# Attention and two expert layers on one core: outer products on other PSUM partitions, wider products for the rest of q, fewer identity products, a new list

## The chip, the cores and the metric

The kernel runs on one core of a Trainium2 chip, in one launch. The metric is the device time of the launch in microseconds (us), lower is better. TensorE (PE in the profile) multiplies, VectorE (DVE), ScalarE (ACT) and GpSimd (POOL) work on elements, and SyncE (SP) issues nearly all transfers from and to HBM, in one queue, in order. Each engine works through its own list of instructions in order and waits for the others by semaphores.

## The reference

```python
# q, k, v: (4, 8, 576, 64); moe_w1, moe_w2: (512, 1024); moe_w3: (1024, 1024); moe_w_out: (1024, 512)
# experts: e_w1 (4, 512, 1024), e_w2 (4, 1024, 512); probs (2304, 4)
kv  = einsum('bhsd,bhse->bhde', k, v)
out = einsum('bhsd,bhde->bhse', q, kv)
out = out / sqrt(mean(out * out, axis=-1) + 1e-6) * g_norm
x = out.transpose(0, 2, 1, 3).reshape(2304, 512)
x = ((x @ w1) * (x @ w2) @ w3) @ w_out
p = probs / (probs.sum(-1, keepdims=True) + 1e-9)
y = sum over e of p[:, e] * (maximum(x @ e_w1[e], 0) @ e_w2[e])
```

The weights of the middle layer arrive as 64-bit floats, as pairs of 32-bit words, and are decoded on ScalarE and VectorE.

## The kernel before

**Attention.** There are 16 *units*, `unit b p`: two heads of one batch. A unit loads q (256 KB) and k and v (288 KB each for batches 0 and 1, which are listed in `NINE`; 256 KB each for batches 2 and 3, and small loads `kvr` of the last 64 tokens). Its steps on TensorE are: outer products k by v (L756 for batches 0 and 1, 18 products; L769 for batches 2 and 3, 12 products), four transposes of q (L724), an inner product of four matmuls of q with the outer product (L804), and, after a normalization, four transposes of the result (L724 again, `ident,x`). Between them ScalarE or VectorE copies the outer products to a tile `kvb` with one block for each head on its diagonal (L788), copies the turned q (L712, L713), squares and sums (L622 or L626, L632); GpSimd takes the root (L639); VectorE scales (L643). In L756 head h uses rows and output partitions 64h to 64h+63. In L769 all 128 rows are tokens, and both heads write partitions 0 to 63, at different columns of the bank:

```python
nc.tensor.matmul(
    ps[0:D, h * D:(h + 1) * D], a, b_, start=r == 0 and h == 0, stop=r == R + 1,
    skip_group_check=True,
)
```

`EARLY` lists the results (in the order of the list) whose squares ScalarE makes in one instruction, with the sum on VectorE; all others are squared and summed on ScalarE in eight pieces of 64 columns.

**Rest of q.** `rest_unit g` does the last 64 tokens of two batches: for each of eight heads and two batches one product of 64 columns with weights of 128 columns (L840), 16 in all.

**Later stages.** The middle layer uses block products of fewer multiplications (`bilinear_plain`, `bilinear_pair`, `mixed_product`, `mixed`); the expert layers follow (L1763 and the three passes of L341 to L343, which multiply float32 numbers split in a high and a low part).

**What sets the order.** `FRONT` is a list of items, written out; each gives operations with an engine and a cost. A planner (`Plan.order`) runs these against modelled engines: the item's place in the list is its priority, an operation is taken when its inputs are ready by the model and a tile is free, and where ScalarE or VectorE could do it, the one that would finish first gets it. So the list and the costs (`cost=` of a load, `{"pe": 1.4}` of the outer products) together fix each engine's order. `FILL` puts products of the identity with itself (L2027) into a fresh PSUM bank, ahead of TensorE's next operation of the stages 1 to 3; `WARM` is the number of such products ahead of everything (L438).

Of the kernel before, what the change touches and what calls it, by code (L numbers as in the profile page):

```python
# [18 lines left out]
P = 128  # L19
# [12 lines left out]
NINE = (0, 1)  # L32
TRAFFIC = 1.02
MARGIN = {"act": 0.1, "dve": 0.1, "sp": 0.2}
EARLY = (2, 3, 4, 5, 8, 15, 16)
WARM = 10
FILL = {1: 3, 2: 3, 3: 2}
START = 0.7
RESERVE = {"h": (5, 2), "b": (1, 1)}
BIAS = {"dve": 1.0, "act": 0.0, "pool": 1.0, "pe": 0.0, "sp": 0.0}  # L40

FRONT = (
# [12 lines left out]
)  # L55

class Buf:
# [210 lines left out]
def attention_moe_kernel(  # L268
# [26 lines left out]
    nc = tc.nc  # L295
# [166 lines left out]
    def decode(name, src, shape=None):  # L462

        raw = Buf("r", name + "raw", [P, 512], I64)
        load(raw, ((lambda t: t.rearrange("p (k f) -> p k f", k=shape)) if shape else whole, src))
        val, add_ = half("val", ring="decoded"), half("add", I32, "decoded")  # L470

        def word(i):
            return raw.tile.bitcast(I32).rearrange("p (n t) -> p n t", t=2)[:, :, i]

        def magnitude(e):
            if e == "act":
                nc.scalar.activation(out=val.tile, in_=word(1).bitcast(F32), func=ACTF.Abs)
            else:
                nc.vector.tensor_scalar(
                    out=val.tile.bitcast(I32), in0=word(1), scalar1=0x7FFFFFFF, scalar2=None, op0=ALU.bitwise_and  # L480
                )

        def rounded(e):
            low = word(0).bitcast(U32)
            if e == "act":
                nc.scalar.activation(out=add_.tile, in_=low, func=ACTF.Copy, scale=2.0 ** -29)
            else:
                nc.vector.tensor_scalar(out=add_.tile, in0=low, scalar1=2.0 ** -29, scalar2=None, op0=ALU.mult)

        def bounded(e):  # L490
            nc.vector.tensor_scalar(
                out=val.tile, in0=val.tile, scalar1=as_float(0x38000000), scalar2=as_float(0x47EFFFFF),
                op0=ALU.max, op1=ALU.min,
            )

        def shifted(e):
            bits = val.tile.bitcast(I32)
            nc.vector.tensor_scalar(
                out=bits, in0=bits, scalar1=3, scalar2=0x3FFFFFFF,
                op0=ALU.logical_shift_left, op1=ALU.bitwise_and,  # L500
            )

        def signed(e):
            bits = val.tile.bitcast(I32)
            nc.vector.scalar_tensor_tensor(
                out=bits, in0=word(1), scalar=-0x40000000, in1=bits, op0=ALU.bitwise_and, op1=ALU.bitwise_or
            )

        def finish(e):
            bits = val.tile.bitcast(I32)  # L510
            nc.vector.tensor_tensor(out=bits, in0=bits, in1=add_.tile, op=ALU.add)

        either = {"act": t_act(512), "dve": t_fast(512)}
        add(either, magnitude, reads=[raw], writes=[val])
        add(either, rounded, reads=[raw], writes=[add_])
        add({"dve": t_fast(512)}, bounded, writes=[val])
        add({"dve": t_fast(512)}, shifted, writes=[val])
        add({"dve": t_dve(512)}, signed, reads=[raw], writes=[val])
        add({"dve": t_dve(512)}, finish, reads=[add_], writes=[val])
        return val  # L520
# [67 lines left out]
    def rest_kv(b, j):  # L588

        turn = sum(at[1] == j for at in kvr) % 2  # L590
        if (turn, j) not in kvr_slots:
            kvr_slots[turn, j] = [half("kvr") for _ in (k, v)]
            for raw in kvr_slots[turn, j]:
                for at in ((REM // 2, REM), (REM, P)):
                    cleared(raw, at)
        kvr[b, j] = kvr_slots[turn, j]
        for raw, src in zip(kvr[b, j], (k, v)):
            load(
                raw,
                (  # L600
                    lambda t: t[0:REM // 2].rearrange("p (h r d) -> p h r d", h=HP, r=2),
                    src[b, j * HP:(j + 1) * HP, M:S, :].rearrange("h (p r) d -> p h r d", r=2),
                ),
                key=0, cost=0.33,
            )

    summed = []
# [121 lines left out]
    def unit(b, p):  # L729
# [3 lines left out]
        loaded = []  # L733
        for name, src in (("q", q), ("kv", k), ("kv", v))[:1 if b in NINE else 3]:
            raw = half(name, ring="attention")
            load(raw, (heads, head_pair(src, b, p)), cost=0.8)
            loaded.append(raw)
        qraw = loaded[0]
        if b in NINE:
            kv = Buf("r", "kv", [P, 2, S], F32)  # L740
            load(kv, *(
                (lambda t, n=n: t[:, n], src[b, 2 * p:2 * p + 2].rearrange("h (g r) d -> (h g) (r d)", g=D))
                for n, src in enumerate((k, v))
            ), cost=1.72)
        else:
            ks, vs = loaded[1:]
            if (b, p // 2) not in kvr:
                rest_kv(b, p // 2)
            kr, vr = kvr[b, p // 2]
# [11 lines left out]
        def outer(e):  # L761
            for r in range(R + 2):
                for h in range(2):
                    if r < R:
                        a, b_ = heads(ks.tile)[:, h, r, :], heads(vs.tile)[:, h, r, :]
                    else:
                        at = (p % 2 * 2 + h) * 2 * D + (r - R) * D
                        a, b_ = kr[:, at:at + D], vr[:, at:at + D]
                    nc.tensor.matmul(  # L769
                        ps[0:D, h * D:(h + 1) * D], a, b_, start=r == 0 and h == 0, stop=r == R + 1,  # L770
                        skip_group_check=True,
                    )

        if b in NINE:
            add({"pe": 1.4}, outer_by_head, reads=[kv], writes=[ps])
        else:
            add({"pe": 0.9}, outer, reads=[ks, vs, kr, vr], writes=[ps])
        own, at = kvb[b][p // 2], p % 2 * 2 * P
        parts = []
        for i in range(2):  # L780
            for h in range(2) if b in NINE else (None,):
                d = slice(i * D, (i + 1) * D)
                n, heads_of = (P, slice(0, 2)) if h is None else (D, slice(h, h + 1))
                rows = slice(0, D) if h is None else slice(h * D, (h + 1) * D)
                parts.append((own, (p, i, h)))
                add(
                    {"act": t_act(n, True), "dve": t_dve(n)},
                    lambda e, d=d, heads_of=heads_of, rows=rows: (  # L788
                        nc.scalar.copy if e == "act" else nc.vector.tensor_copy
                    )(  # L790
                        own[d, at:at + 2 * P].rearrange("p (h c) -> p h c", h=2)[:, heads_of, d],
                        ps[rows, 0:P].rearrange("p (h c) -> p h c", h=2)[:, heads_of],
                    ),
                    reads=[ps], writes=parts[-1:], free=True,
                )
# [18 lines left out]
    def rest_unit(g):  # L814
# [18 lines left out]
        po = bank()  # L833

        def inner(e):
            for h in range(H):
                c = slice(h // 2 * P, (h // 2 + 1) * P)
                for i in range(2):
                    own, at = kvb[2 * g + i][h // 4], h % 4 * P + h % 2 * D
                    nc.tensor.matmul(  # L840
                        po[:, h * D:(h + 1) * D], qs[i][:, c], own[:, at:at + D], start=i == 0, stop=i == 1
                    )

        add({"pe": 1.72}, inner, reads=qs + kvb[2 * g] + kvb[2 * g + 1], writes=[po])
# [1215 lines left out]
```

## Time and profile before

| what | us |
|---|---|
| median of three runs (1115.97 to 1116.68) | 1116.59 |
| profiled execution | 1114.81 |
| its span in the trace | 1113.0 |
| TensorE busy | 1106.1 |
| VectorE busy | 864.4 |
| ScalarE busy | 607.3 |

The span runs from the first to the last instruction of the profiled execution; some 1.8 us lie around it. Records of TensorE overlap (each contains the time in which a product runs through the array), so its busy time tells little, and starts tell when it really issued. A float32 product shows as two records, a transpose as one. A number in brackets behind a row of the list in time is idle time ahead of it and what ended it.

### The profile page before, as it was taken

The page shows a single profiled execution, that of the slowest core. Times are in us where ns is not written, and L with a number is a line of the kernel's source. Part 1 is how long each engine was busy: PE and PEld are TensorE (multiplying, and loading weights), DVE is VectorE, ACT ScalarE, POOL GpSimd, SP SyncE. Part 2 cuts the span into 40 slices and gives each one's busy share as a digit, 9 for nine tenths or more (in the row PEclk, how much of TensorE's full clock was granted, in tenths as well). Part 3 has the DMA queues.
Part 4 walks back from the last instruction along what each step waited for, and adds up shares of the span by engine and source line. Part 5 has one row for each costly group of instructions (what it writes and reads, how often), then busy time and mean ns, then how long its engine had stood idle before and what let it go on. Part 6 is the DMA issues. An engine that isn't in the chain of part 4 may idle for free.

```text
span 1113.0 us, 18828 instructions
## 1 busy us (share of the span) xinstructions
PE 1106.1 (99%) x6577; PEld 1008.8 (91%) x6577; DVE 864.4 (78%) x1692; ACT 607.3 (55%) x1401; POOL 50.9 (5%) x69
## 2 busy tenths in 40 slices
PE   9999999999999999999999999999999999999998
PEld 8888888888888898999989999999999999999998
DVE  4778888988898888888888884567788876485896
ACT  6887636645655665763555465444455555444431
POOL 5521100000000000000000000000000000000000
PEclk9999999999999999999999999999999999999999
DMA  9888979542340399997999997878779967686756
GB/s 316 275 263 266 325 253 331 169 130 79 90 138 1 140 302 339 359 323 256 360 347 350 354 326 268 296 233 295 223 240 338 320 225 249 235 288 221 263 166 196
DMA packets 158723, 282.32 MB, mean 254 GB/s; under 512 B 17316, under 2 KB 65444, under 8 KB 158628
## 3 DMA queue, kind: packets, MB, share of 16 engines
q1 hardware_dynamic: 158464, 280.85, 75.3%
q8 instruction: 52, 0.85, 0.3%
q10 hardware_dynamic: 164, 0.26, 0.1%
q14 instruction: 43, 0.35, 0.1%
HBM read 198.22 MB, written 82.84 MB: 253 GB/s over the span
## 4 chain that ended last, share of the span: by engine, by line
PE 99%; DVE 0%; ACT 0%; issue 0%; POOL 0%; POOLq 0%
PE b L343 25%; PE b L341 25%; PE b L342 25%; PE b L1763 18%; PE b L724 2%; PE b L804 1%; PE b L769 1%; PE b L756 1%; PE b L840 1%; PE b L2027 1%; PE warm L438 0%; ACT x L626 0%; DVE acc L1881 0%; DVE htl L391 0%; DVE acc L1791 0%
## 5 line engine op out<-in xcount | busy, mean ns | idle before, releaser
L712 ACT COPY u<-b 128x384 f32<-128x384 f32 (+1 forms) x193 | 97.9, 507 | 212.6 <-PE b L343 207.1
L1763 PE MATMUL b<-w,hth 128*128 128x512 f32 x588 | 208.4, 394 | 0.1
L1599 DVE TENSOR_TENSOR u<-u,b 128x384 f32<-128x384 f32 x144 | 79.4, 552 | 110.9 <-PE b L343 53.2
L1763 PE MATMUL b<-w,htl 128*128 128x256 f32 x588 | 156.0, 279 | 0.0
L1763 PEld LDWEIGHTS b<-w,hth 128*128 128x128 f32 x588 | 108.9, 188 | 19.7 <-DVE acc L1791 0.5
L1763 PEld LDWEIGHTS b<-w,htl 128*128 128x128 f32 x588 | 110.6, 188 | 3.0
L1791 DVE SCALAR_TENSOR_TENSOR acc<-b,pn,acc 128x512 f32<-128x512 f32 x123 | 85.5, 746 | 29.7 <-PE b L1763 29.5
L386 ACT CAST hth<-s 128x384 fp32r<-128x384 f32 x144 | 69.7, 512 | 44.0 <-DVE s L1699 42.7
L1610 ACT ACTIVATE u<-u 128x384 f32<-128x384 f32 x108 | 56.9, 527 | 45.7 <-DVE u L1599 45.6
L391 DVE TENSOR_TENSOR htl<-s,hth 128x384 fp32r<-128x384 f32 x144 | 75.6, 552 | 5.3 <-ACT hth L386 5.2
L391 DVE TENSOR_TENSOR htl<-u,hth 128x384 fp32r<-128x384 f32 x108 | 56.0, 552 | 3.2 <-ACT hth L386 3.2
L343 PE MATMUL b<-wdh,htl 128*128 128x512 f32 x144 | 56.7, 394 | 0.0
L342 PE MATMUL b<-wdl,hth 128*128 128x512 f32 x144 | 56.6, 393 | 0.0
L341 PE MATMUL b<-wdh,hth 128*128 128x512 f32 x144 | 56.0, 389 | 0.0
L386 ACT CAST hth<-u 128x384 fp32r<-128x384 f32 x107 | 51.2, 509 | 0.4
L341 PE MATMUL b<-w,hth 128*128 128x256 f32 x168 | 47.8, 285 | 0.5 <-DMA w<-w2kept 0.4
L342 PE MATMUL b<-w,hth 128*128 128x256 f32 x168 | 47.5, 283 | 0.0
L343 PE MATMUL b<-w,htl 128*128 128x256 f32 x168 | 47.5, 283 | 0.0
L341 PE MATMUL b<-th,weh 128*128 128x512 f32 x112 | 43.8, 391 | 0.0
L342 PE MATMUL b<-tl,weh 128*128 128x512 f32 x112 | 43.7, 390 | 0.0
L343 PE MATMUL b<-th,wel 128*128 128x512 f32 x112 | 43.6, 389 | 0.0
L1053 DVE TENSOR_TENSOR u<-u,b 128x512 f32<-128x512 f32 x42 | 28.7, 686 | 17.9 <-PE b L343 10.3
(304 smaller groups left out, 3176.4 us busy)
## 6 DMA issues: line engine op xcount, KB each, us to landing
w<-w2kept SPq DMA_DIRECT2D x126, 512.0 KB, 4.9
we<-we SPq DMA_DIRECT2D x240, 256.0 KB, 5.1
we<-weh SPq DMA_DIRECT2D x48, 256.0 KB, 3.8
we<-wel SPq DMA_DIRECT2D x48, 256.0 KB, 3.5
e2raw<-in_moe_w_dram SPq DMA_DIRECT2D x20, 512.0 KB, 5.7
w3raw<-in_moe_w_dram SPq DMA_DIRECT2D x16, 512.0 KB, 3.7
e1raw<-in_moe_w_dram SPq DMA_DIRECT2D x16, 512.0 KB, 5.6
w2kept<-wth SPq DMA_DIRECT2D x32, 256.0 KB, 3.9
```

The lines of the kernel that those rows point to most:

```text
L341: nc.tensor.matmul(ps, w[0], x[0], start=first, stop=False, skip_group_check=more)
L342: nc.tensor.matmul(ps, w[0], x[1], start=False, stop=False, skip_group_check=more)
L343: nc.tensor.matmul(ps, w[1], x[0], start=False, stop=last, skip_group_check=more)
L386: nc.scalar.copy(to(dst.high.tile), value(src.tile))
L391: nc.vector.tensor_tensor(out=to(dst.low.tile), in0=value(src.tile), in1=to(dst.high.tile), op=ALU.subtract)
L712: lambda e: nc.scalar.copy(to(dst.tile), value(src.tile)) if e == "act"
L724: nc.tensor.transpose(ps[:, c], raw[:, c], ident)
L1053: lambda _: nc.vector.tensor_tensor(out=t.tile, in0=t.tile, in1=ps.tile, op=ALU.add),
L1599: lambda _: nc.vector.tensor_tensor(out=t[:, :W], in0=base[:, :W], in1=ps[:, :W], op=ALU.add),
L1610: lambda eng: nc.scalar.activation(out=t[:, :W], in_=src[:, :W], func=ACTF.Relu)
L1763: nc.tensor.matmul(ps.tile if whole_width else ps[:, 0:256], (h.high if whole_width else h.low)[:, c], both if whole_width else raw[:, r, ...
L1791: nc.vector.scalar_tensor_tensor(out=a.tile, in0=ps.tile, scalar=sc, in1=a.tile, op0=ALU.mult, op1=ALU.add)
```

## The change

Five things are edited. The outer products of batches 2 and 3 write head h to output partitions 64h to 64h+63 (`ps[c, c]`), as those of batches 0 and 1 did; all units now share one form of the copies to `kvb`, four of 64x64. `rest_unit` takes two heads at once: 8 products of 128 columns, whose right operand is two blocks of `kvb` at a distance. `FILL` is empty and `WARM` is 7. `EARLY` has ten entries. `FRONT` is a new list, and four planner costs are other numbers (a load of a 64-bit weight 1.4 instead of 1.5, of k and v of a unit of batches 0 and 1 1.53 instead of 1.72, and so on).

```diff
-EARLY = (2, 3, 4, 5, 8, 15, 16)
-WARM = 10
-FILL = {1: 3, 2: 3, 3: 2}
+EARLY = (1, 2, 3, 4, 5, 6, 7, 8, 9, 15)
+WARM = 7
+FILL = {}
 FRONT = (
-    "norm_scale, unit 1 2, unit 1 3, weight 1 4, unit 1 1, weight 1 0, unit 1 0, unit 0 1, unit 0 2, unit "
+    "norm_scale, unit 1 2, weight 1 4, unit 1 0, unit 1 1, weight 1 0, unit 1 3, unit 0 0, unit 0 1, unit "
...
-                    nc.tensor.matmul(
-                        ps[0:D, h * D:(h + 1) * D], a, b_, start=r == 0 and h == 0, stop=r == R + 1,
-                        skip_group_check=True,
-                    )
+                    c = slice(h * D, (h + 1) * D)
+                    nc.tensor.matmul(ps[c, c], a, b_, start=r == 0, stop=r == R + 1)
 
         if b in NINE:
-            add({"pe": 1.4}, outer_by_head, reads=[kv], writes=[ps])
+            add({"pe": 1.27}, outer_by_head, reads=[kv], writes=[ps])
...
-        for i in range(2):
-            for h in range(2) if b in NINE else (None,):
-                d = slice(i * D, (i + 1) * D)
-                n, heads_of = (P, slice(0, 2)) if h is None else (D, slice(h, h + 1))
-                rows = slice(0, D) if h is None else slice(h * D, (h + 1) * D)
-                parts.append((own, (p, i, h)))
+        for h in range(2):
+            for i in range(2):
+                rows, src = slice(i * D, (i + 1) * D), slice(h * D, (h + 1) * D)
+                dst = slice(at + h * P + i * D, at + h * P + (i + 1) * D)
+                parts.append((own, (p, h, i)))
...
-            for h in range(H):
-                c = slice(h // 2 * P, (h // 2 + 1) * P)
+            for h in range(HP):
+                c = slice(h * P, (h + 1) * P)
                 for i in range(2):
-                    own, at = kvb[2 * g + i][h // 4], h % 4 * P + h % 2 * D
+                    own, at = kvb[2 * g + i][h // 2], h % 2 * 2 * P
                     nc.tensor.matmul(
-                        po[:, h * D:(h + 1) * D], qs[i][:, c], own[:, at:at + D], start=i == 0, stop=i == 1
+                        po[:, c], qs[i][:, c],
+                        own[:, at:at + 2 * P].rearrange("p (b c) -> p b c", c=D)[:, 0:4:3], start=i == 0, stop=i == 1,
                     )
```

Lines behind the edits move: L769 is L770 in the changed kernel, L788 is L785, L804 is L798, L840 is L834.

TensorE at the start of the program, before (the names are output<-operands; `q_103` and `kv_107` belong to unit 1 2, `q_116` and `kv_121` to unit 1 3, `q_170` to unit 1 1):

```order
L438 MATMUL warm_86<-ident_72 128x128 x10
L2027 MATMUL b_124<-ident_72 128x128 x3
L724 MATMUL b_124<-ident_72,q_103 128x128 x4
L1950 MATMUL b_137<-ident_72,graw_76 128x1
L2027 MATMUL b_144<-ident_72 128x128 x3
L756 MATMUL b_144<-kv_107 64x64 x18
L2027 MATMUL b_172<-ident_72 128x128 x3
L724 MATMUL b_172<-ident_72,q_116 128x128 x4
L2027 MATMUL b_192<-ident_72 128x128 x3
L756 MATMUL b_192<-kv_121 64x64 x18
L2027 MATMUL b_217<-ident_72 128x128 x3
L804 MATMUL b_217<-kvb_99,qt_135 128x128 x4
```

and with the change (`q_100`, `kv_104`: unit 1 2; `q_125`, `kv_130`: unit 1 0; `q_161`, `kv_166`: unit 1 1; `q_227`: unit 1 3):

```order
L438 MATMUL warm_86<-ident_72 128x128 x7
L724 MATMUL b_118<-ident_72,q_100 128x128 x4
L1945 MATMUL b_135<-ident_72,graw_76 128x1
L756 MATMUL b_137<-kv_104 64x64 x18
L724 MATMUL b_173<-ident_72,q_125 128x128 x4
L798 MATMUL b_185<-kvb_96,qt_127 128x128 x4
L756 MATMUL b_196<-kv_130 64x64 x18
L724 MATMUL b_229<-ident_72,q_161 128x128 x4
L756 MATMUL b_242<-kv_166 64x64 x18
L798 MATMUL b_271<-kvb_94,qt_194 128x128 x4
L724 MATMUL b_283<-ident_72,q_227 128x128 x4
```

The identity groups between the units' groups are gone, and unit 1 0 stands second instead of unit 1 3.

SyncE's queue of loads at the start, before (`q_103`, `q_116`, `q_170`: as above; `w2raw_139` is `weight 1 4`):

```order
L363 DMA q_103<-in_q_dram 128x2x256
L363 DMA kv_107<-in_k_dram 128x576
L363 DMA kv_107<-in_v_dram 128x576
L363 DMA q_116<-in_q_dram 128x2x256
L363 DMA kv_121<-in_k_dram 128x576
L363 DMA kv_121<-in_v_dram 128x576
L363 DMA w2raw_139<-in_moe_w2_dram 128x2x256
L363 DMA q_170<-in_q_dram 128x2x256
```

and with the change (`w2raw_113`: `weight 1 4`; `q_125`: unit 1 0; `q_161`: unit 1 1):

```order
L363 DMA q_100<-in_q_dram 128x2x256
L363 DMA kv_104<-in_k_dram 128x576
L363 DMA kv_104<-in_v_dram 128x576
L363 DMA w2raw_113<-in_moe_w2_dram 128x2x256
L363 DMA q_125<-in_q_dram 128x2x256
L363 DMA kv_130<-in_k_dram 128x576
L363 DMA kv_130<-in_v_dram 128x576
L363 DMA q_161<-in_q_dram 128x2x256
```

The first weight moves from behind the second unit's loads to ahead of them.

## Rows read from the trace of the kernel before

**Rows 1.** The page's busy times: us (share of the span) and instructions.

```profile
PE 1106.1 (99%) x6577; PEld 1008.8 (91%) x6577; DVE 864.4 (78%) x1692; ACT 607.3 (55%) x1401; POOL 50.9 (5%) x69
```

**Rows 2.** TensorE's waits, whole span: for whom, total us, times, longest us.

```profile
PE warm L438 <- POOL ident masks.py:199: 1.3, 1, 1.3
PE b L804 <- ACT kvb L788: 0.6, 1, 0.6
PE b L341 <- DMA w<-w2kept: 0.4, 1, 0.4
```

**Rows 3.** TensorE in order of time, 0 to 45 us: start, us, what, records.

```profile
1.34 4.51 PE L438 MATMUL warm<-ident 128*128 128x128 f32 x20 [1.34 <-POOL ident masks.py:199]
5.69 0.83 PE L2027 MATMUL b<-ident 128*128 128x128 f32 x6
...
7.04 0.94 PE L2027 MATMUL b<-ident 128*128 128x128 f32 x6
7.90 1.26 PE L756 MATMUL b<-kv 64*64 64x64 f32 x36
...
22.30 0.83 PE L2027 MATMUL b<-ident 128*128 128x128 f32 x6
22.98 0.60 PE L724 MATMUL b<-ident,x 128*128 128x128 f32 x4
23.50 1.26 PE L756 MATMUL b<-kv 64*64 64x64 f32 x36
24.70 0.66 PE L724 MATMUL b<-ident,q 128*128 128x128 f32 x4
```

**Rows 4.** The same view: the first outer products of batches 2 and 3.

```profile
32.01 1.15 PE L769 MATMUL b<-kv 128*64 128x64 f32 x16
32.99 0.63 PE L769 MATMUL b<-kvr 128*64 128x64 f32 x8
33.55 0.66 PE L724 MATMUL b<-ident,x 128*128 128x128 f32 x4
```

**Rows 5.** The same view, 86 to 92 us: the first rest of q.

```profile
87.01 1.05 PE L804 MATMUL b<-kvb,qt 128*128 128x128 f32 x8
87.89 3.68 PE L840 MATMUL b<-kvb,qr 128*128 128x64 f32 x32
91.39 0.48 PE L341 MATMUL b<-xth,weh 128*128 128x512 f32 x1
```

**Rows 6.** SyncE's queue in order of time: four issues, start and us.

```profile
1.73 0.43 SPq L363 DMA_DIRECT2D kv<-in_v_dram  x1
...
3.68 0.43 SPq L363 DMA_DIRECT2D w2raw<-in_moe_w_dram  x1
...
5.91 0.42 SPq L363 DMA_DIRECT2D w2raw<-in_moe_w_dram  x1
...
18.51 0.33 SPq L363 DMA_DIRECT2D kv<-in_v_dram  x1
```

**Rows 7.** The same four issues among the DMA issues: KB, us to landing.

```profile
kv<-in_v_dram SPq DMA_DIRECT2D x1, 288.0 KB, 4.2
...
w2raw<-in_moe_w_dram SPq DMA_DIRECT2D x1, 512.0 KB, 6.2
...
w2raw<-in_moe_w_dram SPq DMA_DIRECT2D x1, 512.0 KB, 9.6
...
kv<-in_v_dram SPq DMA_DIRECT2D x1, 288.0 KB, 6.1
```

**Rows 8.** Busy us by stretch: PE, PEld, DVE, ACT, POOL; granted clock, DMA share, GB/s.

```profile
20.00:80.00 60.00, 60.00 (x609) 53.15 (x608) 47.83 (x87) 51.02 (x182) 26.41 (x31) 1.00 0.88 273
80.00:140.00 60.00, 60.00 (x364) 51.97 (x364) 47.05 (x88) 41.61 (x128) 12.09 (x12) 1.00 0.88 296
...
1108.00:1113.00 5.00, 0.62 (x6) 0.42 (x4) 0.59 (x2) 0.00 (x0) 0.00 (x0) 0.85 0.49 157
```

More of the change, by code (lines that the diff above doesn't have):

```diff
@@ L468, in decode @@
         raw = Buf("r", name + "raw", [P, 512], I64)
-        load(raw, ((lambda t: t.rearrange("p (k f) -> p k f", k=shape)) if shape else whole, src))
+        load(raw, ((lambda t: t.rearrange("p (k f) -> p k f", k=shape)) if shape else whole, src), cost=1.4)
         val, add_ = half("val", ring="decoded"), half("add", I32, "decoded")
@@ L603, in rest_kv @@
                 ),
-                key=0, cost=0.33,
+                key=0, cost=0.3,
             )
@@ L735, in unit @@
             raw = half(name, ring="attention")
-            load(raw, (heads, head_pair(src, b, p)), cost=0.8)
+            load(raw, (heads, head_pair(src, b, p)), cost=0.75)
             loaded.append(raw)
@@ L743, in unit @@
                 for n, src in enumerate((k, v))
-            ), cost=1.72)
+            ), cost=1.53)
         else:
@@ L779, in unit @@
         parts = []
-        for i in range(2):
-            for h in range(2) if b in NINE else (None,):
-                d = slice(i * D, (i + 1) * D)
-                n, heads_of = (P, slice(0, 2)) if h is None else (D, slice(h, h + 1))
-                rows = slice(0, D) if h is None else slice(h * D, (h + 1) * D)
-                parts.append((own, (p, i, h)))
-                add(
[L787 to L792, printed above, removed]
+        for h in range(2):
[3 more added lines that the diff above has]
+                parts.append((own, (p, h, i)))
+                add(
+                    {"act": t_act(D, True), "dve": t_dve(D)},
+                    lambda e, rows=rows, src=src, dst=dst: (nc.scalar.copy if e == "act" else nc.vector.tensor_copy)(
+                        own[rows, dst], ps[src, src]
                     ),
```

22 rows, old and new, of the table FRONT are left out of this document.

## The prediction

> **What bounds the kernel now.** I read the busy shares first [rows 1]: TensorE 99% of a 1113.0 us span, VectorE 78%, ScalarE 55%. Records of matmuls overlap, so a busy share proves little by itself; the waits of TensorE come next [rows 2]. In the whole span it waits three times: 1.3 us for the identity at the start, 0.6 us for a copy into kvb, 0.4 us for a load. Third, the list in order of time: from the first product at 1.34 us each group starts where the one before it has been issued, with no hole [rows 3 to 5]. So the end is the sum of TensorE's issue times, and the reader should look at the distance between starts, not at the length of a record. Other engines matter only if they make TensorE wait. Product records below are of float32 products, which the profile shows twice (10 warm products are x20); transposes show once.
>
> **The change, part by part.** The set of products on TensorE is the same before and after except for four groups; all else is moved by the new list.
>
> *Identity products between groups.* Eight groups of x6 go. One takes 0.68 us to the next start (22.30 to 22.98), the longest kind 0.86 us (7.04 to 7.90) [rows 3]; all eight distances add up to 5.9 us.
>
> *Warm products.* The x20 take 1.34 to 5.69, 0.217 us each [rows 3]; three fewer products are six records: 1.3 us.
>
> *Outer products of batches 2 and 3 (L769).* A unit has 24 records and takes 32.01 to 33.55 = 1.54 us, 0.064 us each; eight units, 12.3 us [rows 4]. Now the second head writes partitions 64 to 127, so the two heads stand in different columns of the array. The trace doesn't show that form. The lower bound of the gain is nothing: stream and weights are as large as before, which is also why I exclude a loss. The upper bound is the pace of L756, whose heads are apart in rows and columns: 36 records in 23.50 to 24.70, 1.20 us, 0.033 us each [rows 3]. 24 of these are 0.80 us, a gain of 0.74 us a unit, 5.9 us in all. I take that end, because L756 is the nearest row: same type, same 64 columns of stream and of weights, two heads in turn.
>
> What speaks against it is the weight load. L840 streams 64 columns at 3.50/32 = 0.109 us, no faster than L804 streams 128 (0.88/8 = 0.110) [rows 5]; both load 128 columns of weights, so the load sets L840's pace, and by the same rate 64 columns need about 0.055 us, close to what L769 takes. Packing must therefore run two loads side by side, too, and in L769 and its successor both heads use all 128 rows. The Trainium skill ("TensorE: Matmul & The Clock Gate", Part 3) says that a weight load overlaps running products only where the row group differs; by that sentence this term would be 0 and the sum 5.9 us smaller. It also says in "TensorEngine Tiling (Array Packing)", Key Properties, that tiles load and multiply independently, which leaves the term at 5.9 us. The trace bears the first out only in part: L804's loads stand in the same rows as its products and still don't slow them [rows 5].
>
> *Rest of q.* 32 records of 64 columns take 87.89 to 91.39, 3.50 us [rows 5]; there are two such units, 7.0 us. Instead there are 16 records of 128 columns each, at L804's 0.110 us: 1.76 us. Gain 2 x 1.73 = 3.5 us. This is the surest term: same weights, half as many loads.
>
> Together 5.9 + 1.3 + 5.9 + 3.5 = 16.6 us of TensorE's work.
>
> *What comes back: waits at the beginning.* The identity products stood where data was late. I place loads by their bytes, in the new order of the queue, on landings of before: 832 KB at 1.73 + 4.2 = 5.9 us, 2176 KB at 3.68 + 6.2 = 9.9, 3520 KB at 5.91 + 9.6 = 15.5, 6848 KB at 18.51 + 6.1 = 24.6 [rows 6, 7]. Steps of TensorE from [rows 3, 5]: four transposes 0.5 us, 18 outer products 1.2, an L804 group 0.9. Seven warm products end at 1.34 + 14 x 0.217 = 4.4. The first transposes follow at half pace (about 1.0), then 0.5 us of waiting for k and v; the outer products end at 7.2. The second unit's q is now behind a weight (1600 KB): 8.2, a wait of 1.0. Transposes and an inner product to 9.6; k and v (2176 KB) 9.9, a wait of 0.3; to 11.1. The third q (2432 KB) is there; k and v (3008 KB) land at 13.4, after 11.6: 1.8. Outer and inner product to 15.5; the fourth q (3776 KB) at about 16.6 by the slower rate, or 16.2 by the faster: 1.1. From here on a unit's 832 KB arrive in 2.3 us, while TensorE needs 3.1 for it, so loads lead again. Waits 4.7, slow transposes 0.5: 5.2 us come back, and the 0.6 us wait of before goes. Bounds: 2.2 us, if loads run at the faster rate from 5.9 us on (waits 0.5, 0.8, 0.2 and 0.2, and 0.5 for the transposes), to some 8 us, if 3 us of products run at half the clock as well.
>
> *Clock.* The warm products run at 0.217 us a record, the 1.2 GHz level, the identity groups at 0.112, the 2.4 GHz one; the rise comes just before 5.69, after TensorE worked without a hole from 1.34 [rows 3]. In the new list it works until 5.4. The only fall in the trace is at the end: the last 5 us have a mean granted clock of 0.85, that is half the clock for 1.5 us, so some 3 us after the last product [rows 8]. My longest new wait is 1.8 us, so I charge nothing more.
>
> *ScalarE, VectorE, GpSimd.* Eight units' two copies of 64x128 become four of 64x64, and three more units square in one ScalarE instruction, with a reduction on VectorE. None of it is on TensorE's path as long as TensorE finds other work; the cover is thinner than before, since between 20 and 80 us VectorE is busy 47.8 and ScalarE 51.0 of 60 us [rows 8].
>
> **Sum.** Off 16.6 + 0.6, back 5.2, and 1 us for waits in the re-listed front after 20 us (an estimate; the trace has 0.4 us of that kind): 11.0 us net. The profiled execution took 1114.8 us (span 1113.0), so 1103.8 on that scale; the median of the three runs, 1116.6, is 1.8 above it: **1105.6 us**. With the bounds of the waits alone 1102 to 1109.
>
> **Rivals.**
> *The heads don't overlap.* The weight loads in the same rows take turns, L770 keeps 0.064 us a record, and that part of the change does nothing. This is what the first sentence of the Trainium skill named above would make of it. For it: the load floor above. Against it: L756. 5.9 us less gain: 1111.5, in 1108 to 1115.
>
> *ScalarE and VectorE stay at their share.* From 20 to 80 us they do 98.9 us of work in 120. TensorE would now finish that stretch in about 52 us (the lead of 2.6 us from the beginning and seven units of L769), which asks for 95% of both. If they only hold their 82%, the stretch stays 60 us and up to 8 us become waits; some is made good later, where 80 to 140 us are less crowded. 6 us lost: 1111.6, in 1109 to 1114.
>
> *The clock falls.* If a wait between 7 and 17 us becomes long enough, products run at 1.2 GHz until it rises; as at the start that is some 4.3 us at double length: 2 to 4 us more, 1109.
>
> *Slower than before.* The same engines, with worse interleaving: if their common share in that stretch falls to 70%, 98.9 us of work need 70.6 instead of 52 us, 18 us of new waits, 1124. It decides from 75% on (66 us, 14 us lost). Against it: before held 82% with a full TensorE, and the work there is nearly the same.
>
> **How the numbers follow.** Forecast 62%; no overlap 14%; share held 14%; clock 5%; slower 5%. Below 1101.5 the waits would have to be under 2 us in all, some 7%; above 1112.5 lie parts of the second and third case and the last, about 13%. So 1101.5 to 1112.5. What a measurement can tell from no change is 0.2%, 2.2 us. Forecast and clock case are faster by more than that, so is most of the second and third: 0.89; within it 0.05; slower 0.06.
>
> **What would show it.** L770: pairs of starts some 0.06 us apart, 0.8 us a unit, if right, 1.5 if not. L834: two groups of x16, 1.8 us each. TensorE's waits: some 5 us before 17 us, for loads of q and kv; the first group of the outer products of batches 2 and 3, at 32.01 before, starts earlier by some 3 us against the groups around it that are the same. Wrong would be: waits of TensorE for ScalarE or VectorE after 20 us of over 3 us, product records with the double distance after 6 us, or the same total with L770 at the old pace.

## The result and the profile after

The changed kernel takes 1107.38 us (median of four, 1105.63 to 1108.19) against 1116.28 for the kernel before: ratio 0.9919, interval 0.9902 to 0.9936. 8.9 us less; forecast were 11.0, and 1107.4 lies in the range. The profiled execution fell from 1114.81 to 1107.7 us, its span from 1113.0 to 1105.9: 7.1 us.

The page's busy times after, beside [rows 1]:

```profile
PE 1094.7 (99%) x6491; PEld 995.0 (90%) x6491; DVE 863.9 (78%) x1692; ACT 609.2 (55%) x1375; POOL 54.7 (5%) x69
```

TensorE is still at 99%, but it waits more than before. Its waits after (for whom, total us, times, longest), beside [rows 2]:

```profile
PE b L341 <- ACT u L712: 2.6, 3, 1.6
PE b L756 <- DMA kv<-in_v_dram: 2.4, 2, 2.1
PE warm L438 <- POOL ident masks.py:199: 1.3, 1, 1.3
PE b L724 <- DMA q<-in_q_dram: 0.2, 1, 0.2
PE b L1758 <- DVE acc L1786: 0.2, 1, 0.2
```

The beginning after, TensorE in order of time (start, us, what, records, idle ahead), beside [rows 3]:

```profile
1.34 3.35 PE L438 MATMUL warm<-ident 128*128 128x128 f32 x14 [1.34 <-POOL ident masks.py:199]
4.49 1.06 PE L724 MATMUL b<-ident,q 128*128 128x128 f32 x4
5.48 0.26 PE L1945 MATMUL b<-ident,graw 1*128 1x1 f32 x1
7.86 2.18 PE L756 MATMUL b<-kv 64*64 64x64 f32 x36 [2.12 <-DMA kv<-in_v_dram]
10.27 1.12 PE L724 MATMUL b<-ident,q 128*128 128x128 f32 x4 [0.23 <-DMA q<-in_q_dram]
11.18 1.91 PE L798 MATMUL b<-kvb,qt 128*128 128x128 f32 x8
13.02 1.44 PE L756 MATMUL b<-kv 64*64 64x64 f32 x36
14.39 0.66 PE L724 MATMUL b<-ident,q 128*128 128x128 f32 x4
14.97 1.26 PE L756 MATMUL b<-kv 64*64 64x64 f32 x36
16.17 1.16 PE L798 MATMUL b<-kvb,qt 128*128 128x128 f32 x8
```

Two things are to be seen: TensorE waits 2.1 us for the first v, and the products from 7.86 to about 13.4 us run at half pace, the 1.2 GHz level. (The granted clock is on record only from a trace's first change on, here the rise at 13.4 us. The column reads 1.00 ahead of that, as it does for the slow warm products before, so there the distance of starts has to tell the level.) 36 outer products take some 2.2 us at 7.86 and 1.20 at 14.97; the inner product's eight records take 1.84 us at 11.18 (to 13.02) and 0.99 at 16.17.

The outer products of batches 2 and 3 (beside [rows 4]) and the rest of q (beside [rows 5]), the same view after:

```profile
34.92 0.69 PE L770 MATMUL b<-kv 128*64 128x64 f32 x16
35.44 0.40 PE L770 MATMUL b<-kvr 128*64 128x64 f32 x8
35.77 0.66 PE L724 MATMUL b<-ident,x 128*128 128x128 f32 x4
...
84.20 1.95 PE L834 MATMUL b<-kvb,qr 128*128 128x128 f32 x16
85.90 0.48 PE L341 MATMUL b<-th,weh 128*128 128x512 f32 x1
```

A unit's outer products take 0.85 us instead of 1.54, the rest of q 1.70 instead of 3.50. Both edits do on TensorE what was forecast. A marker further on tells how the saving is spread: the first product of the expert stage, before and after,

```profile
390.69 0.34 PE L341 MATMUL b<-x11h,weh 128*128 128x384 f32 x1
```

```profile
382.44 0.34 PE L341 MATMUL b<-x11h,weh 128*128 128x384 f32 x1
```

So 8.25 us are gained ahead of it, and 1.1 us are lost behind it. Eight times 0.69 and twice 1.80 make 9.1 us; 1.9 us are lost in one hole at 144 us, shown next; what is left for all the rest is about 1.1 us of the 7.2 that identity and warm products cost. The hole, on TensorE and ScalarE, and SyncE's queue ahead of it:

```profile
144.36 0.39 PE L343 MATMUL b<-th,wel 128*128 128x512 f32 x1
146.31 0.50 PE L341 MATMUL b<-th,weh 128*128 128x512 f32 x1 [1.56 <-ACT u L712]
```

```profile
145.18 1.07 ACT L712 COPY u<-b 128x512 f32<-128x512 f32 x2 [3.88 <-DMA ab1kept<-u]
```

```profile
129.13 0.66 SPq L446 DMA_DIRECT2D praw<-in_moe_domain_probs_dram  x1
...
134.13 0.47 SPq L451 DMA_DIRECT2D praw<-in_moe_domain_probs_dram  x1
...
140.89 0.90 SPq L376 DMA_DIRECT2D ab1kept<-u  x2
```

TensorE waits for a bank that a ScalarE copy empties; the copy waits until a store (`ab1kept`) has read the tile that it writes; and SyncE had spent 129.1 to 134.7 us on the eight small loads of the experts' shares. Before, these eight stood at 295 us. The new list has moved `expert_shares` from the 63rd place to the 35th, and the planner books its eight loads at 1.0 us.

### The profile page after: what moved, and what is told of

It is laid out like the page before. It is cut to its first block, busy times and chain, and to the rows that moved or that the text cites. A ratio compares the mean times of both kernels' runs of the same rounds, so it can differ in the third digit from the quotient of the medians.

```text
span 1105.9 us, 18648 instructions
## 1 busy us (share of the span) xinstructions
PE 1094.7 (99%) x6491; PEld 995.0 (90%) x6491; DVE 863.9 (78%) x1692; ACT 609.2 (55%) x1375; POOL 54.7 (5%) x69
## 4 chain that ended last, share of the span: by engine, by line
PE 94%; DMA 4%; SPq 1%; DVE 1%; ACT 0%; issue 0%; ACTq 0%
PE b L341 24%; PE b L343 24%; PE b L342 24%; PE b L1758 19%; PE b L724 2%; PE b L798 1%; DMA kv<-in_k_dram 1%; DMA kv<-in_v_dram 1%; DMA e2raw<-in_moe_w_dram 1%; PE b L770 1%; SPq L363 0%; PE b L756 0%; DMA we<-weh 0%; DMA ab1kept<-u 0%; DMA ab0kept<-u 0%; PE b L834 0%
```

## The experiments

Each kernel was measured beside the kernel before; differences below are between medians of one group. The first group edits the changed kernel.

**The changed kernel again.**

> The changed kernel as it is, as the measure for the other three of this group. Both theories expect 1107.4 us, within 1.5. In the first trace of it the clock rose to its upper level only at 13.4 us (in the kernel before at 5.6) and TensorE waited 1.9 us at 144 us, 1.0 at 536 and 0.5 at 649 for ScalarE copies. If these belong to the new list, they stand here again; if they are chance of one execution, they are elsewhere or gone.

1107.38 us (1106.19 to 1108.94). The hole at 144 us is there again (2.1 us over the usual distance), the first v is late again; the waits at 536 and 649 us are gone, and one of 0.4 us stands at 525. The clock behaves otherwise, as three stretches of this trace show (busy us of PE, PEld, DVE, ACT, POOL; granted clock, DMA share, GB/s):

```profile
5.80:9.00 3.20, 1.26 (x36) 1.16 (x36) 0.16 (x1) 0.37 (x1) 2.98 (x6) 1.00 0.97 326
9.20:15.90 6.70, 5.99 (x54) 5.32 (x56) 2.71 (x4) 5.19 (x27) 3.52 (x6) 0.50 1.06 387
16.00:20.00 4.00, 3.97 (x59) 3.71 (x58) 2.16 (x4) 3.35 (x9) 1.43 (x3) 1.00 1.05 371
```

It rose before the first outer products, fell at 9.1 us, and stayed at the 1.2 GHz level until 15.9. So a slow stretch belongs to this beginning, and its place changes. In all seven traces with 7 warm products some products between 6 and 16 us ran at half pace; behind the warm products of the seven traces with 10 or 16, none did before 200 us.

**More warm products.**

```diff
-WARM = 7
+WARM = 16
```

> 16 warm products instead of 7, nothing else: TensorE then has no hole before the first k and v are there, and the clock should rise near 5.6 us instead of 13.4. Theory A (the late clock is paid for): the products between 7.9 and 13.4 us run at full pace, 2.5 us less, 1105 us. Theory B (the loads of q, k and v set the pace up to some 22 us, since there outer products start within 0.2 us of the landing of their v): the clock rises early and the total stays within 0.7 us of the unedited one.

1105.90 us, 1.5 less (ratios to before 0.9907 and 0.9922, with intervals that overlap a little). The trace has no stretch at half pace behind the warm products, and no wait for a load. It isn't the loads that keep the gain below the slow products' 3.0 us: the first v lands at 6.6 us, but sixteen warm products stand ahead of the first transposes until 7.9, so the first outer products start later than the 7.86 above, though at full pace:

```profile
8.59 1.26 PE L756 MATMUL b<-kv 64*64 64x64 f32 x36
```

From there to 21.5 us of the first trace 2.3 us are won, after 0.7 lost; TensorE is 1.5 us ahead. It loses 0.9 of that to a wait for VectorE at 65.6 us, and at the first product of the expert stage it is 0.2 us ahead of the first trace of the changed kernel and 1.2 of the second. So theory B falls and the late clock does cost, but that the total shows 1.5 us as well is partly chance. A number of warm products that ends as v lands was not run with these edits.

**The heads back on the same partitions.**

```diff
-                    c = slice(h * D, (h + 1) * D)
-                    nc.tensor.matmul(ps[c, c], a, b_, start=r == 0, stop=r == R + 1)
+                    nc.tensor.matmul(
+                        ps[0:D, h * D:(h + 1) * D], a, b_, start=r == 0 and h == 0, stop=r == R + 1,
+                        skip_group_check=True,
+                    )
...
```

> The changed kernel with both heads of the outer products of batches 2 and 3 on partitions 0 to 63 again, all orders and the four copies kept. If TensorE's issue time sets the end there, the 192 records take 12.2 instead of 6.8 us and the total rises by 5.4 us, to 1112.8. If other engines or loads bind in that stretch (20 to 107 us), the rise is under 3 us.

1113.72 us (1110.45 to 1115.45), 6.3 more. TensorE's issue time binds there; the packing is worth what it saves. The records make 5.4 us of it; in the trace another 0.6 us is a longer hole, in which TensorE waits 2.6 us for ScalarE instead of 2.0.

**The rest of q back in 64 columns.**

```diff
-            for h in range(HP):
-                c = slice(h * P, (h + 1) * P)
+            for h in range(H):
+                c = slice(h // 2 * P, (h // 2 + 1) * P)
...
```

> The changed kernel with the rest of q in products of 64 columns again, 16 for a unit, all orders kept. If TensorE's issue time sets the end, 64 records at 0.109 us instead of 32 at 0.110: 3.5 us more, 1110.9. If something else binds there, under 2 us.

1107.98 us (1106.81 to 1109.41): only 0.6 more, a miss for the sum. The records do cost 3.5 us (two groups of x32), but TensorE's waits have no ScalarE in them any more:

```profile
PE b L724 <- DMA q<-in_q_dram: 1.7, 1, 1.7
PE b L756 <- DMA kv<-in_v_dram: 1.4, 1, 1.4
PE warm L438 <- POOL ident masks.py:199: 1.3, 1, 1.3
PE b L341 <- DMA w<-w2kept: 0.2, 1, 0.2
```

The hole at 144 us is gone: ScalarE's copy ahead of it starts 4.2 us later than in the first trace of the changed kernel (144.94 instead of 140.71), SyncE's store only 1.3 us (142.17 instead of 140.89). In the new list most of the wider products' gain is handed back there: against the second trace this one is 3.7 us behind at 105 us and 1.5 at 147 and at the end. The 0.6 us of the medians is uncertain by more than 1 us.

The second group edits the kernel before.

**No identity products between groups.**

```diff
-FILL = {1: 3, 2: 3, 3: 2}
+FILL = {}
```

> The kernel before without the identity products between the groups, nothing else; ten warm products stay. If they only stood in TensorE's way, 5.9 us less: 1110.4. If they mostly covered waits for loads (theory B), TensorE waits instead and the total falls by 1 to 3.5 us, to 1113 to 1115, with waits for loads of q, k and v before 25 us. If they were needed to keep the clock up, it rises late or falls and the total stays within 1 us or grows.

1111.87 us against 1115.83: 4.0 less, between the two forecasts. The products take 5.9 us; waits for loads take some of their place (2.2 us for a q at 16 us, 0.9 for a v at 8.6):

```profile
PE b L724 <- DMA q<-in_q_dram: 2.2, 1, 2.2
PE warm L438 <- POOL ident masks.py:199: 1.3, 1, 1.3
PE b L341 <- ACT u L712: 1.3, 2, 0.8
PE b L756 <- DMA kv<-in_v_dram: 0.9, 1, 0.9
...
```

The profiled execution (1113.6 us) is the slowest of the five; at 130 us it is 2.9 us ahead of the trace of before. With its ten warm products it ran at full pace from 4.5 us to the last product, so the identity groups weren't needed for the clock.

**Packing alone.** The edit of L769 and the four copies, in the old list.

> The kernel before with only the outer products of batches 2 and 3 on different partitions, with the four copies of 64x64 that this needs. If the sum of issue times holds: 5.4 us less, 1110.9. If the old list lets ScalarE and VectorE take it back: under 3 us less.

1109.46 us, 6.4 less, the same as its price in the new list, and again some 1 us more than the records give (5.4). Part of that may be order: with four copies to place, the planner exchanges some of TensorE's groups from 34 us on.

**The four edits, old list.** Packing, 128 columns, no identity groups, 7 warm products; `FRONT`, `EARLY` and the costs of before.

> The kernel before with its old list, old EARLY and old costs, and the four edits of TensorE's work: packed outer products, rest of q in 128 columns, no identity products, 7 warm products. If the list as such is worth little, this takes 1107 to 1109 us like the changed kernel. If the new list is what makes the edits pay, it takes over 1110. If the new list costs (its waits after 140 us), it takes under 1106.

1102.26 us (1101.51 to 1102.48): 13.6 less than before (ratio 0.9876) and 5.1 less than the changed kernel (0.9922). The first product of the expert stage starts at

```profile
378.22 0.34 PE L341 MATMUL b<-x11h,weh 128*128 128x384 f32 x1
```

4.2 us ahead of the changed kernel's, and TensorE's waits are short:

```profile
PE warm L438 <- POOL ident masks.py:199: 1.3, 1, 1.3
PE b L341 <- ACT u L712: 1.2, 1, 1.2
PE b L756 <- DMA kv<-in_v_dram: 0.7, 1, 0.7
...
```

**The new list alone.** The changed kernel with the four edits taken back.

> The changed kernel with all four edits of TensorE's work taken back (unpacked outer products, rest of q in 64 columns, identity products between groups, 10 warm products); the new list, EARLY and costs stay. If the list as such is neutral: 1116 us. If it brings waits of its own after 140 us, some 3 us more than before: 1119. If it is a gain by itself: under 1114.

1115.25 us (1113.29 to 1118.46), ratio to before 0.9995, interval 0.9986 to 1.0004: neutral. TensorE's groups stand in the same order as in the changed kernel, but the hole at 144 us isn't there. So the list costs nothing as long as TensorE's work is long, and 5.1 us when it is short.

The third group tests the hole, and the repairs.

**The shares' loads later.** The eight loads and the four VectorE instructions that use them are taken out of the planned order and put back 60 places later in SyncE's queue.

```diff
...
+        moved = [o for o in ordered if o[0].emit in (load_probs, shares)]
+        later = [i for i, o in enumerate(ordered) if i >= first and o[1] == "sp"][60]
+        ordered[later:later] = moved
...
```

> The changed kernel with the eight small loads of the experts' shares, and the four VectorE instructions on them, 60 places later in SyncE's queue; every other order is kept. In the changed kernel these eight take SyncE from 129.1 to 134.7 us, and behind them stand the stores of ab1kept that a ScalarE copy waits for when TensorE stops at 144 us. If SyncE's queue sets that wait, it is gone and the total falls by some 2 us, to 1105.5. If the copy waits for something else (TensorE's own results, the transfers' bandwidth), the wait stays and the total within 0.7 us of 1107.4.

1111.06 us, 3.7 more: a miss in the total, though the hole at 144 us is gone as expected (no wait over 0.15 us between 80 and 200 us). The edit has made a new one. The waits between 205 and 217 us:

```profile
DVE total L455 <- DMA praw<-in_moe_domain_probs_dram: 4.5, 1, 4.5
...
PE b L341 <- DVE u L1048: 4.0, 1, 4.0
```

In its new place the loads had just been issued when VectorE came to the sum of the shares; it waited 4.5 us, in order, and TensorE behind it 4.0. Then TensorE's products stood at twice the usual distance for a while:

```profile
216.36 0.80 PE L341 MATMUL b<-xth,weh 128*128 128x512 f32 x1 [3.98 <-DVE u L1048]
216.95 0.63 PE L342 MATMUL b<-xtl,weh 128*128 128x512 f32 x1
217.38 0.63 PE L343 MATMUL b<-xth,wel 128*128 128x512 f32 x1
```

That is 0.43 us from start to start where 0.23 is usual. The granted clock stood at half until 222.1 us (columns as above):

```profile
216.40:219.00 2.60, 2.60 (x6) 2.11 (x7) 2.04 (x4) 0.00 (x0) 0.00 (x0) 0.50 0.00 0
219.00:222.00 3.00, 3.00 (x15) 2.91 (x14) 1.94 (x4) 0.62 (x1) 0.00 (x0) 0.50 0.56 175
```

The wait cost 4.1 us and the slow clock behind it 2.5. Less the 1.9 us of the old hole that is 4.7, and this execution's span is 4.8 us longer than the first one's of the changed kernel. It is the slowest of the five (1112.5 us); the 3.7 is the difference of the medians.

**The same with the rest of q in 64 columns.**

> The same with the rest of q in 64 columns again. With the shares in their old place this edit cost 0.6 us and not 3.5, and the wait at 144 us was gone with it. If SyncE's queue took the rest of it there, the edit costs its full price now: 3.5 us more than late_shares, 1109. If the price of the wider products was wrong, the difference stays near 0.6 us.

1114.85 us (1112.36 to 1116.61): 3.8 more than with 128 columns. The price is right; the shares' place decides whether it arrives at the end. (The two profiled executions differ by 1.4 us in span only: in the stretch of the edit itself, between 80 and 106 us, the one with 64 columns falls back by 3.6, but it had lost 2.2 us less up to there, 1.8 of them at the beginning, loses 1.0 less to the slow clock behind the wait at 212 us, and 0.9 more later on.)

**Both repairs.**

> late_shares with 16 warm products: the two repairs together. If they add up: 2.0 + 1.5 us off 1107.4, 1104. If the time gained at the beginning is lost again at 144 us, 1105.5.

1110.14 us, 0.9 less than with the shares alone. It can't tell more, since the new hole at 212 us is in it.

**The old list with the four edits and 16 warm products.**

> The old list with the four edits of TensorE's work (1102.3 us with 7 warm products, where the clock rose at 10.0 us) and 16 warm products. If the late clock costs there as in the new list: 1.0 to 1.5 us less, 1101. If loads bind in the first 20 us, within 0.5 us of 1102.3.

1101.88 us (1101.65 to 1102.44), ratio 0.9872, interval 0.9859 to 0.9885: the fastest of all, but 0.4 us from the one with 7 warm products is no clear difference. The first and the third unit's outer products, with 7 warm products and then with 16:

```profile
6.42 2.18 PE L756 MATMUL b<-kv 64*64 64x64 f32 x36 [0.67 <-DMA kv<-in_v_dram]
...
13.35 1.26 PE L756 MATMUL b<-kv 64*64 64x64 f32 x36
```

```profile
7.92 1.26 PE L756 MATMUL b<-kv 64*64 64x64 f32 x36
...
13.31 1.26 PE L756 MATMUL b<-kv 64*64 64x64 f32 x36
```

Sixteen warm products make the first outer products 1.5 us later and all that follows faster; at 13.3 us the two traces are level. So here the nine further warm products themselves take the early clock's gain. Behind that the landing of a q sets the pace (waits of 0.2 and 0.8 us).

## Why the prediction was right, and where not

**What bounds.** Right. Where an edit makes TensorE's list shorter and nothing else late, the end moves by about as much: 6.3 and 6.4 us for the packing (5.4 by the records), 3.8 for the rest of q (3.6).

**Packing.** Right, at 5.4 us by the records (0.85 us a unit, forecast 0.80) against 5.9. The rule cited against it, that a weight load overlaps running products only where the row group differs ("TensorE: Matmul & The Clock Gate", Part 3, in the Trainium skill), would have left 0.064 us a record; 24 records in 0.85 us are 0.035, with all 128 rows used by both heads. The trace speaks for the other sentence of the Trainium skill, that tiles load and multiply independently ("TensorEngine Tiling (Array Packing)", Key Properties). The edit changes the columns of the array and the output partitions together, so the runs don't tell whether loading or writing was the limit. The rival without overlap has fallen.

**Rest of q.** Right in TensorE's time (3.6 us), wrong in what it brings in this kernel: 0.6 us by the medians, 1.5 by the traces. The forecast costed an edit without asking which engine meets TensorE next at that place; the answer was SyncE's queue at 129 to 141 us.

**Identity and warm products, and what comes back.** The term was mis-sized: 2.6 us were forecast for the beginning, about 2.1 stayed (7.2 and 0.6 less 3.0 for half pace and 2.7 of waits, see below), and 0.9 us went further on, where nothing was forecast. Distances from start to start, added up by line to the first product of the expert stage, give: 16.2 us less for what was removed or packed; 3.1 more for transposes of q, outer products of batches 0 and 1 and inner products, nearly all of it half pace; 3.7 more of waits; 1.2 more for the products of 128x512, 0.3 of it at the hole. Most of the other 0.9 are changes of kind: such a product takes 0.31 to 0.34 us to the next start right behind a group of transposes, outer or inner products, and 0.23 elsewhere, and the new list changes more often. Two steps of the forecast for the beginning failed. The first is the placing of loads by the bytes ahead of them. The first v has the same bytes ahead of it in both lists and was put at 5.9 us. After, with a weight behind it in the queue instead of a q:

```profile
kv<-in_v_dram SPq DMA_DIRECT2D x1, 288.0 KB, 6.0
```

issued at 1.72, landed at 7.7. In fourteen traces (five with the old list, nine with the new) it landed at 5.7 to 6.3 us with the old list and at 6.6 to 7.7 with the new, whatever the number of warm and identity products. So what stands *behind* a load counts as well. The loads after it were late too: the second unit's q was put at 8.2 us and landed at 10.2, its v at 9.9 and 11.7. The Trainium skill ("DMA: Bandwidth & Descriptors", Two DMAs through the same engine are not ordered) says that nothing orders transfers across the sixteen engines; it gives no delay for that. In these fourteen traces the first loads still landed in the order of their issue, so none shows a load overtaking another; how a load behind the first v delays it stays open.

The second is the clock. Beyond 0.5 us for the first transposes it was put down at nothing, because the longest wait was thought to be 1.8 us; more was left to the upper bound of the waits and to the rival with a chance of 5%. Products at double distance after 6 us were even named as a sign of being wrong, and they came. They ran at half pace for some 5 us, and with the first transposes that cost some 3.0 us (1.0 for the outer products at 7.86, 0.9 for the inner at 11.18, 0.4 and 0.5 for two groups of transposes, 0.2 after 13.02). Waits were only 2.7 us instead of 4.7, which fits a slower TensorE that comes to its loads later. The sum of both, 5.7, was near the forecast's 5.2 by luck; the split was wrong.

**Later waits.** Forecast 1 us, found 2.6 in the waits for ScalarE, 1.6 of it at 144 us. This is the largest error of the sum. The part at 144 us is the list's: the old list with the four edits has no wait there. The rest isn't, since that kernel waits 1.2 us for ScalarE at 518 us; waits of that kind change from one execution to the next. Of the 5.1 us between the lists, 4.2 are there at the first product of the expert stage: 1.9 for the hole, 1.1 for longer waits in the first 22 us, 0.8 for more changes of kind, 0.4 in smaller parts. The products at half pace cost the same with both lists, though the clock was up at 10.0 us instead of 13.4. About 1 us lies behind, in waits of the expert stage that differ as much between two executions of one kernel. These parts are read from one trace of each; no run takes them apart.

**Rival of the full vector engines.** Fallen. From 20 to 80 us of the changed kernel (columns as above):

```profile
20.00:80.00 60.00, 59.69 (x633) 51.72 (x629) 50.67 (x94) 53.39 (x168) 30.32 (x29) 1.00 0.95 295
```

VectorE and ScalarE do 104.1 us of work in 120, 87%, where [rows 8] had 82%, and TensorE waits 0.3 us, for a load.

## What to carry to other kernels

When the bound engine has hardly a hole, price an edit by the distance between starts, then ask at the next two or three meeting points at which queue that engine will now arrive too early; a gain of 3.5 us can end in one store. After making work shorter, try the old order first: here it was 5 us better than the new one, and one edit at a time told which part carried the gain. A list of many small transfers costs its issue time (4.4 to 5.6 us for eight here), wherever it stands, and moving it needs a look at who uses the data next. The number of warm products deserves runs of its own: seven left half pace behind them, sixteen held the first outer products back by 0.7 and 1.5 us.

## What was not expected of the hardware

Two heads whose products use the same rows but other columns of the array, and so other output partitions, issue at 0.035 us a record against 0.064 in the same columns, weight loads included.

In the second trace of the changed kernel the granted clock fell to the 1.2 GHz level at 9.1 us, 0.4 us into a wait of 1.2 us, with a wait of 1.7 us and 1.3 us of products ahead of it. It stayed there until 15.9, though TensorE was busy for 6.0 us of that time. In the first trace of the same program it rose once, at 13.4. With the shares' loads later, the wait of 4.0 us at 212 us was followed by products at that level for 5.7 us; with the rest of q in 64 columns as well, the fall came only 1.1 us after products had begun again.

The landing of one load moved with what was queued behind it: 6.1 us in the median with the old list, 7.0 with the new.
